# The opening of a fused transformer block: the silu(c) row read in PSUM, low parts made in pieces, and one written sequence for the queues

## The chip, the cores and the metric

The kernel runs on one NeuronCore of a Trainium2 chip (trn2). The metric is the device time of one execution in microseconds. Engines are named as in the profile: PE is the matrix engine (PEld its weight loads), DVE the vector engine, ACT the scalar engine, POOL the general one (GpSimd), and SP is the queue that issues the DMAs.

## The reference

One block on x of 2048 rows by 1024: a modulation from a conditioning row c, an attention with a memory over four segments of 512 rows (32 heads of 32), and a gated feed-forward of width 3584. All of it is float32.

```python
mod = (silu(c) @ w_mod).reshape(1, 6, 1, 1024)      # sa, ca, ga, sb, cb, gb
h = layernorm(x) * (1 + ca) + sa
q, k, v = h @ wq, h @ wk, h @ wv                    # 32 heads, 4 segments of 512
for s in range(4):
    p = softmax(qs @ ks.T * scale + mask)
    o = g * (phi(qs) @ M) / (phi(qs) @ z + 1e-6) + (1 - g) * (p @ vs)
    M, z = M + phi(ks).T @ vs, z + sum(phi(ks))
x = x + ga * (o @ wo)
h = layernorm(x) * (1 + cb) + sb
x = x + gb * ((gelu(h @ w_gate) * (h @ w_up)) @ w_down)
```

## The kernel before, in words

**Numbers.** Matrix products need more than one pass: an operand is split into a high part, rounded to the format of the fast pass, and a low part, the rest. A product is then high by high, low by high and high by low. ACT or DVE makes a high part with a cast, POOL or DVE makes the low part with a subtraction (on POOL in pieces of 256 columns).

**Stages.** The opening prepares segment 0 and projects it for the first group of four heads. Then come 33 steps of attention (for two halves, eight groups, two segments each), the output projection, and the feed-forward. In a step n the scores S of one group and segment are made, the second half T of the step before, and the projection K (keys and values) and Q of the step after. Inside a step a row of short names (`ORDER`) says in which sequence the pieces are written; all five queues take them in that sequence.

**The opening.** `modT` is a table of 48 columns of 128: column r = 8j + kt belongs to part j of the modulation (0 the shift sa, 1 the scale ca) and to the kt-th block of 128 channels. A column is made on DVE (`mod_col`, L159): w_mod's block r, 128 by 1024, times the row silu(c), spread over all partitions (`scb`), summed along the row; for a scale 1.0 is added (L164). The row itself is made by PE: ones times a diagonal of silu(c) (`row_parts`, L124 to L131), two halves in PSUM, copied by ACT to `scb`. Two of the 16 columns of the opening are made as products on PE instead (`mod_mm`, L170), from a block that the host has turned.

Segment 0 comes as x tiles of 128 rows. Their norm (`norm_stats`, L216 to L222: DVE's statistics, POOL's power -0.5; L1472 and L1475: the scaling on ACT) is followed by `norm_seg` (L311 to L329): for each kt PE turns four blocks into a PSUM bank (`tpa`), ACT makes h from it with the scale column and the shift column of this kt (L318), then come its high part `hha` and low part `hla`. `first_part` (L496, L499) takes kt after kt as they come and accumulates keys, values (`kv`) and queries (`q`) in three PSUM banks; it ends by copying them out (`kn` on ACT, `vx` on DVE), and by the pieces after it: `kt` turns the keys (kT) and splits them, `qo` splits the queries (qh, ql), `dk` and `dq` spread both by DMA into ks and qs, `ek`, `ea` and `eb` make phi.

Segment 1 does the same inside the opening's end and step 0. w_mod's blocks come in pairs (`pair(kt)`: scale and shift) into eight buffers, the first four pairs ahead of everything else, the others as buffers come free. Weights of the first group are rk, rq and rv; their high and low parts are w. The opening is recorded with its instructions in the written order on each queue. The 8 PSUM banks are: 2 for `mm`, 1 for `o`, 5 for `s` (turned blocks, scores, products of columns).

The opening's core, as written before:

```python
mod_col(*got[8])
scaled(0, 3, (0,), x0)
next(nseg)
mod_col(*got[0])
W[0][1] = split_w(raw0[1], wsp_tile("w0_1"), nc.vector)
next(nseg)
W[0][0] = split_w(raw0[0], wsp_tile("w0_0"))
...
for kt in range(1, KT + 1):
    ...
    (mod_mm if kt in (1, 7) else mod_col)(*got[8 + kt])
    mod_col(*got[kt])
    next(nseg)
```

Of the kernel before, what the change touches and what calls it, by code (L numbers as in the profile page):

```python
# [11 lines left out]
F32 = mybir.dt.float32  # L12
# [7 lines left out]
P = 128  # L20
D = 1024
# [15 lines left out]
def block_kernel(ctx: ExitStack, tc: tile.TileContext, x, c, wmod, wq, wkv, wo, beta, wg, wu, wd, out):  # L37
# [81 lines left out]
    def row_parts(dst, cols, tmp, name):  # L119

        dgs = []
        for h in range(2):
            dg = tmp(f"{name}dg{h}")
            nc.vector.tensor_tensor(dg.rearrange("p (k m) -> p k m", m=P), ident.unsqueeze(1).to_broadcast([P, 4, P]),  # L124
                                    cols[:, 4 * h:4 * h + 4].unsqueeze(2).to_broadcast([P, 4, P]), op=ALU.mult)
            dgs.append(dg)
        yield
        for h in range(2):
            ps = s_ps(f"{name}{h}")
            nc.tensor.matmul(ps, ones, dgs[h], start=True, stop=True)  # L130
            nc.scalar.activation(dst[:, h * L:(h + 1) * L], ps, AF.Copy)  # L131
            yield
# [25 lines left out]
    def mod_col(r, w, behind=False):  # L158
        i = nc.vector.tensor_tensor_reduce(out=w, in0=w, in1=scb, scale=1.0, scalar=0.0,  # L159
                                           op0=ALU.mult, op1=ALU.add, accum_out=modT[:, r:r + 1])  # L160
        if behind:
            hold(i)
        if r // 8 in (1, 4):
            nc.vector.tensor_scalar_add(modT[:, r:r + 1], modT[:, r:r + 1], 1.0)  # L164

    def mod_mm(r, w):

        ps = s_ps(f"col{r}")
        for k in range(KT):
            nc.tensor.matmul(ps[:, :1], w[:, k * P:(k + 1) * P], scol[:, k:k + 1], start=(k == 0), stop=(k == KT - 1))  # L170
        nc.scalar.activation(modT[:, r:r + 1], ps[:, :1], AF.Identity, bias=1.0)

# [10 lines left out]

    def load_w(src, name):
        return split_w(fetch(src, name), wsp_tile("w" + name))

# [115 lines left out]
    def norm_seg(s, halves):  # L302

        hs = hT[s] = []
        turned = []

        def turn(kt):
            if kt < KT:
                ps = s_ps(f"tpa{s}_{kt}")
                for i in range(4):  # L310
                    nc.tensor.transpose(ps[:, i * P:(i + 1) * P], halves[kt // 4][i][:, (kt % 4) * P:(kt % 4 + 1) * P], ident)  # L311
                turned.append(ps)

        turn(0)
        yield
        for kt in range(KT):
            h = tmp_tile(f"h{s}_{kt}")
            nc.scalar.activation(h, turned[kt], AF.Identity, bias=modT[:, kt:kt + 1], scale=modT[:, 8 + kt:9 + kt])  # L318
            hi = hT_tile(f"hha{s}_{kt}", s)
            lo = hT_tile(f"hla{s}_{kt}", s)  # L320
            if s:
                nc.vector.tensor_copy(hi, h)
            else:
                nc.scalar.activation(hi, h, AF.Copy)
            if s and kt % 2 == 0:
                nc.vector.tensor_sub(lo, h, f32(hi))
            else:
                for k in (0, L // 2):
                    nc.gpsimd.tensor_sub(lo[:, k:k + L // 2], h[:, k:k + L // 2], f32(hi[:, k:k + L // 2]))  # L329
            hs.append((hi, lo))  # L330
            turn(kt + 1)
            yield
# [148 lines left out]
    def first_part(n, g, s):  # L481
# [22 lines left out]
        yield  # L504
        for q in "kt dk ek qo dq ea eb".split():
            u[q]()
# [279 lines left out]
    def feed_forward():  # L786
# [547 lines left out]
        for m in range(NCH):  # L1334
# [33 lines left out]
        (0,):  # L1368
            "K N K G1 N K N K G2 N G0 K K S0 K S1 C1 K S2 l1 K C2 S3 L1 l2 tm tq A tr L2 K",
        (1,):  # L1370
            "T0 K0 K1 D0 ns K2 T1 rt nc P0 mz m0 nu dn K3 T2 n0 n1 o0 Q0 Q1 T3 nd S0 ne nl m1 P2 S1 rm S2 K4 "
            "Q2 S3 yt tm Q3 K5 K6 K7 tq wl qo o1 zs tr dq A kt ea eb dk ek",
# [46 lines left out]
    proj = projections()  # L1419
    gab = []  # L1420
    def opening():
        x0 = [[], []]
# [15 lines left out]
        def x1_load(i):  # L1438
            x1h.append(fetch(x[L + i * P:L + (i + 1) * P, :], f"x1_{i}"))

# [6 lines left out]
        pair(3)  # L1447
        x1_load(0)

# [39 lines left out]
        W[0] = [None, None, None]
        nseg = norm_seg(0, x0)  # L1490
        mod_col(*got[8])
        scaled(0, 3, (0,), x0)
        next(nseg)
        mod_col(*got[0])
        W[0][1] = split_w(raw0[1], wsp_tile("w0_1"), nc.vector)
        next(nseg)
        W[0][0] = split_w(raw0[0], wsp_tile("w0_0"))
        scaled(0, 0, (1,), x0)
        scaled(0, 1, (1,), x0)
        first = first_part(0, 0, 0)  # L1500
        nseg1 = None
        for kt in range(1, KT + 1):
            if kt < KT:
                if kt + 3 < KT:
                    pair(kt + 3)
                    if kt in (1, 2, 3):
                        x1_load(kt)
                (mod_mm if kt in (1, 7) else mod_col)(*got[8 + kt])
                mod_col(*got[kt])
                next(nseg)  # L1510
            if kt == 1:
                W[0][2] = split_w(raw0[2], wsp_tile("w0_2"))
                scaled(0, 2, (1,), x0)
                scaled(0, 3, (1,), x0)
            if kt == 3:
                x1h = [[t[:, h * L:(h + 1) * L] for t in x1h] for h in range(2)]
                nseg1 = norm_seg(1, x1h)
            if 3 <= kt < 7:
                stats(1, kt - 3, x1h)
            if 4 <= kt < 8:  # L1520
                scaled(1, kt - 4, (0, 1), x1h)
            next(first)
        next(nseg1)
        next(first)
        next(nseg1)
        next(nseg1)
        next(first)
        next(nseg1)
        next(nseg1)
        return x1h, nseg1  # L1530

# [146 lines left out]
```

## Time and profile before

| | us |
|---|---|
| median of 3 runs | 2776.51 (2775.17 to 2778.23) |
| the profiled execution | 2774.08 |
| its span, first to last instruction | 2772.4 |
| PE busy | 2725.8 |
| DVE, ACT, POOL busy | 1568.4, 1204.0, 888.9 |

A row of the timeline gives the start and the duration in us, the engine, the line, the operation, the tiles out<-in, the shape and how many instructions were merged; in brackets stands the idle time ahead of it and whose instruction ended it. A row of a table of windows gives the window, its length, then busy time (and count) of PE, PEld, DVE, ACT and POOL, the granted PE clock, the DMA share and GB/s. A row of a group gives count, busy time and mean ns, then idle time ahead. A row of a tile gives minimum, median and maximum in ns. A row of DMA issues gives the count, the size and the median us to landing.

### The profile page before, as it was taken

The page shows a single profiled execution, that of the slowest core. Times are in us where ns is not written, and L with a number is a line of the kernel's source. Part 1 is how long each engine was busy: PE and PEld are TensorE (multiplying, and loading weights), DVE is VectorE, ACT ScalarE, POOL GpSimd, SP SyncE. Part 2 cuts the span into 40 slices and gives each one's busy share as a digit, 9 for nine tenths or more (in the row PEclk, how much of TensorE's full clock was granted, in tenths as well). Part 3 has the DMA queues.
Part 4 walks back from the last instruction along what each step waited for, and adds up shares of the span by engine and source line. Part 5 has one row for each costly group of instructions (what it writes and reads, how often), then busy time and mean ns, then how long its engine had stood idle before and what let it go on. Part 6 is the DMA issues. An engine that isn't in the chain of part 4 may idle for free.

```text
span 2772.4 us, 43014 instructions
## 1 busy us (share of the span) xinstructions
PE 2725.8 (98%) x14748; PEld 2286.4 (82%) x14748; DVE 1568.4 (57%) x3519; ACT 1204.0 (43%) x2806; POOL 888.9 (32%) x1448
## 2 busy tenths in 40 slices
PE   7999999999999999999999999999999999999999
PEld 6798888888888777778888878888888888888887
DVE  7677667766676735655555445333433244475456
ACT  5677777776767624334322323111111033233323
POOL 5333334533333533344555552444351000000000
PEclk8999999999999999999999999999999999999999
DMA  6455444435443558778898778999999687796563
GB/s 228 135 147 151 113 145 137 134 100 147 121 130 100 149 183 273 243 293 302 321 340 322 267 267 279 341 362 362 353 361 329 215 303 264 259 307 207 179 206 127
DMA packets 244890, 637.77 MB, mean 230 GB/s; under 512 B 24768, under 2 KB 49344, under 8 KB 244672
## 3 DMA queue, kind: packets, MB, share of 16 engines
q1 hardware_dynamic: 244672, 635.03, 67.5%
q8 instruction: 116, 1.90, 0.3%
q14 instruction: 102, 0.84, 0.1%
HBM read 372.79 MB, written 211.81 MB: 211 GB/s over the span
## 4 chain that ended last, share of the span: by engine, by line
PE 89%; DVE 4%; issue 2%; POOL 2%; DMA 1%; ACT 1%; SPq 0%; POOLq 0%; ACTq 0%; DVEq 0%
PE f L1107 35%; PE y L1306 19%; PE kv L367 12%; PE q L373 6%; PE y L690 4%; PE S L524 3%; PE T L615 3%; PE O L627 3%; PE num L583 1%; PE M L566 1%; PE tpb L250 0%; POOL t L827 0%; PE R L633 0%; PE kT L401 0%; PE kv L496 0%
## 5 line engine op out<-in xcount | busy, mean ns | idle before, releaser
L1107 PE MATMUL f<-A,B 128*128 128x512 f32 x4704 | 1075.0, 390 | 3.6 <-DVE c L1127 1.5
L1107 PEld LDWEIGHTS f<-A,B 128*128 128x128 f32 x4704 | 880.8, 188 | 190.8 <-DVE c L1119 2.8
L1306 PE MATMUL y<-B,L 128*128 128x512 f32 x2352 | 533.3, 389 | 0.0
L1306 PEld LDWEIGHTS y<-B,L 128*128 128x128 f32 x2352 | 441.4, 188 | 91.7
L528 ACT ACTIVATE sj<-sj,mm 128x384 f32<-128x384 f32 (+3 forms) x512 | 281.4, 552 | 52.6 <-DVE mm L526 52.0
L526 DVE CUSTOM_DVE_ANT_0 sj<-S,mask 128x384 f32<-128x384 f32 (+3 forms) x512 | 227.9, 488 | 109.7 <-PE S L524 85.5
L618 POOL TENSOR_SCALAR_AFFINE_SELECT pt<-pt 128x128 f32<-128x128 f32 x512 | 165.3, 345 | 295.0 <-ACT pt L617 288.4
L821 ACT ACTIVATE L<-X 128x512 fp32r<-128x512 f32 x168 | 105.8, 630 | 258.6 <-PE y L1306 167.9
L617 ACT ACTIVATE pt<-T 128x256 f32<-128x256 f32 (+3 forms) x512 | 182.0, 445 | 66.0 <-PE T L615 58.8
L367 PE MATMUL kv<-w,hhh 128*128 128x256 f32 x1024 | 199.6, 285 | 0.0
L823 DVE TENSOR_TENSOR L<-X,L 128x512 fp32r<-128x512 f32 x168 | 116.0, 692 | 146.2 <-ACT L L821 146.1
L1130 ACT ACTIVATE g<-g 128x512 f32<-128x512 f32 x56 | 35.3, 631 | 339.9 <-DVE g L1129 339.9
L358 POOL TENSOR_TENSOR w<-r,w 128x256 fp32r<-128x256 f32 x180 | 133.1, 771 | 155.3 <-ACT w L352 153.7
L367 PE MATMUL kv<-w,hha 128*128 128x256 f32 x896 | 177.0, 285 | 0.0
L1046 POOL TENSOR_TENSOR rw<-rw,gbb 128x256 f32<-128x256 f32 x112 | 91.6, 853 | 247.4 <-DMA rw<-wd 166.5
L367 PEld LDWEIGHTS kv<-w,hhh 128*128 128x128 f32 x1024 | 164.8, 191 | 1.4 <-issue 0.4
L367 PEld LDWEIGHTS kv<-w,hha 128*128 128x128 f32 x896 | 145.6, 191 | 2.0 <-issue 0.8
L367 PE MATMUL kv<-w,hlh 128*128 128x256 f32 x512 | 144.7, 283 | 0.0
L690 PE MATMUL y<-wo,hho 128*128 128x512 f32 x384 | 125.7, 394 | 1.7 <-DVE xr L694 1.7
L367 PE MATMUL kv<-w,hla 128*128 128x256 f32 x448 | 126.9, 283 | 0.0
L1123 ACT ACTIVATE g<-f 128x512 f32<-128x512 f32 x56 | 33.5, 598 | 206.5 <-PE f L1107 206.5
L615 PE MATMUL T<-qs,ks 128*128 128x256 f32 (+2 forms) x512 | 108.3, 334 | 7.5 <-DVE qs L543 4.6
(244 smaller groups left out, 4215.4 us busy)
## 6 DMA issues: line engine op xcount, KB each, us to landing
bc_d<-B SPq DMA_DIRECT2D x189, 512.0 KB, 5.4
B<-bc_d SPq DMA_DIRECT2D x189, 512.0 KB, 5.4
B<-wc_d SPq DMA_DIRECT2D x112, 512.0 KB, 3.8
hid_d<-g SPq DMA_DIRECT2D x56, 512.0 KB, 4.3
wc_d<-T SPq DMA_DIRECT2D x56, 512.0 KB, 7.0
X<-hid_d SPq DMA_DIRECT2D x112, 256.0 KB, 4.9
wr<-gd_d SPq DMA_DIRECT2D x84, 256.0 KB, 4.0
ks<-kh SPq DMA_DIRECT2D x64, 256.0 KB, 3.6
```

Source lines behind the costliest of these rows:

```text
L358: nc.gpsimd.tensor_sub(w[:, 1, c], r[:, c], f32(w[:, 0, c]))
L367: nc.tensor.matmul(ps, b[:, sl], w[:, a], start=(kt == 0 and a == 0 and b is hi), stop=(kt == KT - 1 and a == 1), **kw)
L373: nc.tensor.matmul(ps, w[:, a], b, start=(kt == 0 and a == 0 and b is hi), stop=(kt == KT - 1 and a == 1), **kw)
L526: nc.vector.tensor_tensor_reduce(out=sj[:, :nv], in0=ps[:, :nv], in1=mask[:, L - nv:], scale=-1.0, scalar=3.4e38, op0=ALU.add, op1=ALU.min ...
L528: nc.scalar.activation(sj[:, :nv], sj[:, :nv], AF.Exp, bias=mm[:, j, i:i + 1], scale=-1.0, accum_out=ll[:, i, j:j + 1])
L615: nc.tensor.matmul(ps[:, :nn], ks[:, j, kc * P:(kc + 1) * P], qs[:, j, L - nn:], start=True, stop=True)
L617: nc.scalar.activation(pt, ps[:, nn - n:nn], AF.Exp)
L618: nc.gpsimd.affine_select(pt[:, :P], pt[:, :P], pattern=[[1, P]], compare_op=ALU.is_ge, fill=0.0, base=0, channel_multiplier=-1)
L690: nc.tensor.matmul(ps, b[:, i * P:(i + 1) * P], w[:, a, g % 2], start=(g == 0 and a == 0 and b is hi), stop=(g == G - 1 and a == 1))
L823: eng.tensor_sub(lo[:, k], src[:, k], f32(hi)[:, k])
L1107: nc.tensor.matmul(ps, B[m, i][:, a, kt * P:(kt + 1) * P], A[p, i, kt][b], start=(start and kt == 0 and a == 0 and b == 0), stop=(kt == 3 ...
L1306: nc.tensor.matmul(banks[t], ops[k][:, y, t * P:(t + 1) * P], B[slots[k]][:, x], start=(i not in (2, 4, 3) and j == 0 and x == 0 and y == ...
```

## The change

Seven things change, all in the opening and steps 0 and 1.

- The row silu(c) stays in PSUM as well: `scp`, two banks. `mod_col` reads it there for the opening's 16 columns (r below 16). ACT still copies it to `scb`, which the later columns read.
- For this the `s` banks are 3 in the opening; at the unit `S` the two banks are given back and `s` has 5 again.
- The low parts of wq's and of the value half's weights are written in pieces (`split_parts`), each a unit of its own.
- The opening is one written sequence of units, `OPENING`, with a name for each: `s` and `t` statistics, `a` and `b` scaling, `r` the row, `C` and `c` a scale and a shift column, `K`, `q`, `v` the weights' splits, `p` and `x` loads, `n` and `N` a kt of `norm_seg` for segment 0 and 1, `F` a kt (or end) of `first_part`.
- The columns made as products on PE are r = 6 and 15, where they were 9 and 15; the first x tile of segment 1 is loaded later.
- In segment 1, ACT makes the high parts of kt 0, 2, 3, 4 and 6 (DVE made all eight), and DVE the low parts of kt 0, 1, 5, 6 and 7 (it made 0, 2, 4 and 6).
- Step 0 has another row in `ORDER`, step 1 has `K0` ahead of `T0`, and the pieces after a `first_part` stand in another order (`AFTER`).

```diff
+    small = [*psum_pool("begin"), 3]
+    scp = small[0].tile([P, D], F32, name="scp")
     def s_ps(name):
-        return psum.tile([P, L], F32, name=name, tag="s", bufs=5)
+        return small[0].tile([P, L], F32, name=name, tag="s", bufs=small[2])
+
+    def s_all():
+        small[1]()
+        small[:] = [*psum_pool("small"), 5]
+        ctx.callback(small[1])
...
-            ps = s_ps(f"{name}{h}")
+            ps = scp[:, h * L:(h + 1) * L] if name == "sc" else s_ps(f"{name}{h}")
...
     def mod_col(r, w, behind=False):
-        i = nc.vector.tensor_tensor_reduce(out=w, in0=w, in1=scb, scale=1.0, scalar=0.0,
+        i = nc.vector.tensor_tensor_reduce(out=w, in0=scp if r < 16 else w, in1=w if r < 16 else scb, scale=1.0, scalar=0.0,
...
+    def split_parts(r, w):
+        nc.scalar.activation(w[:, 0], r, AF.Copy)
+        yield
+        for k in range(0, 1024, 256):
+            nc.gpsimd.tensor_sub(w[:, 1, k:k + 256], r[:, k:k + 256], f32(w[:, 0, k:k + 256]))
+            yield
...
-            if s:
+            if kt in HI_DVE[s]:
...
-            if s and kt % 2 == 0:
+            if kt in LO_DVE[s]:
...
-        for q in "kt dk ek qo dq ea eb".split():
+        for q in AFTER[s].split():
...
         (0,):
-            "K N K G1 N K N K G2 N G0 K K S0 K S1 C1 K S2 l1 K C2 S3 L1 l2 tm tq A tr L2 K",
+            "N K K N G1 K N N G2 K G0 K S0 S1 C1 S2 K S3 C2 K l1 l2 A tm tr tq L1 K K L2 K",
...
+    AFTER = ('qo kt ek dq ea dk eb', 'kt qo ea eb dk dq ek')
+    HI_DVE = ((), (1, 5, 7))
+    LO_DVE = ((), (0, 1, 5, 6, 7))
+    BY_PRODUCT = (6, 15)
+    OPENING = (
+        "s0 s1 a2 r r s2 a5 r q s3 a6 a4 a0 c0 C1 C0 K q n n a3 v p4 c1 q q C2 c3 c2 n p5 v C4 C3 F c5 n F q "
+        "c4 F x0 v p6 p7 v a7 a1 C5 n v x1 t0 C6 n n F x2 c6 n x3 C7 c7 b0 t1 t2 F F n b1 F t3 F b2 S b3 F F "
+        "N N N N N ")
```

On POOL, from the last norm of segment 0 to the low part of kt 4, this stood before (`w_0` from rq and `w_2` from rv are the weights, `rsa` a norm's power, x2 and x4 count pieces):

```order
L222 TENSOR_TENSOR rsa_3_230<-rsa_3_230,mhalf 128x1
L329 TENSOR_TENSOR hla_0_253<-h_0_250,hha_0_252 128x256 x2
L181 TENSOR_TENSOR w_0_262<-rq_141,w_0_262 128x256 x4
L329 TENSOR_TENSOR hla_1_288<-h_1_285,hha_1_287 128x256 x2
L181 TENSOR_TENSOR w_2_297<-rv_145,w_2_297 128x256 x4
L378 MEMSET vx_0_306 128x4x2
L378 MEMSET vx_1_668 128x4x2
L329 TENSOR_TENSOR hla_2_336<-h_2_333,hha_2_335 128x256 x2
L329 TENSOR_TENSOR hla_3_370<-h_3_367,hha_3_369 128x256 x2
L222 TENSOR_TENSOR rsa_0_384<-rsa_0_384,mhalf 128x1
L329 TENSOR_TENSOR hla_4_410<-h_4_407,hha_4_409 128x256 x2
```

And this stands there now:

```order
L200 TENSOR_TENSOR w_0_187<-rq_145,w_0_187 128x256
L345 TENSOR_TENSOR hla_0_260<-h_0_257,hha_0_259 128x256 x2
L200 TENSOR_TENSOR w_0_187<-rq_145,w_0_187 128x256 x2
L345 TENSOR_TENSOR hla_1_283<-h_1_280,hha_1_282 128x256 x2
L200 TENSOR_TENSOR w_2_189<-rv_149,w_2_189 128x256
L394 MEMSET vx_0_300 128x4x2
L345 TENSOR_TENSOR hla_2_324<-h_2_321,hha_2_323 128x256 x2
L200 TENSOR_TENSOR w_0_187<-rq_145,w_0_187 128x256
L200 TENSOR_TENSOR w_2_189<-rv_149,w_2_189 128x256 x2
L345 TENSOR_TENSOR hla_3_380<-h_3_377,hha_3_379 128x256 x2
L200 TENSOR_TENSOR w_2_189<-rv_149,w_2_189 128x256
L238 TENSOR_TENSOR rsa_0_397<-rsa_0_397,mhalf 128x1
```

The eight pieces of weights have been spread among the low parts of h; the low part of kt 2 stands behind four of them where it stood behind all eight.

On DVE, this stood from scale column 2 on (each column is an ISA row with its read of the sum behind it; a TENSOR_SCALAR follows a scale column only):

```order
L159 ISA wm_c,modT<-wm_c,scb 128x1024
L159 ISA modT 128x1
L164 TENSOR_SCALAR modT<-modT 128x1
L159 ISA wm_c,modT<-wm_c,scb 128x1024
L159 ISA modT 128x1
L159 ISA wm_d,modT<-wm_d,scb 128x1024
L159 ISA modT 128x1
L164 TENSOR_SCALAR modT<-modT 128x1
L159 ISA wm_d,modT<-wm_d,scb 128x1024
L159 ISA modT 128x1
```

And now, from the same column on:

```order
L171 ISA wm_c,modT<-scp,wm_c 128x1024
L171 ISA modT 128x1
L176 TENSOR_SCALAR modT<-modT 128x1
L171 ISA wm_d,modT<-scp,wm_d 128x1024
L171 ISA modT 128x1
L171 ISA wm_c,modT<-scp,wm_c 128x1024
L171 ISA modT 128x1
L171 ISA wm_a,modT<-scp,wm_a 128x1024
L171 ISA modT 128x1
L176 TENSOR_SCALAR modT<-modT 128x1
L171 ISA wm_d,modT<-scp,wm_d 128x1024
```

The shift column 3 (`wm_d` without an addition behind it) has moved ahead of shift column 2, and scale column 4 (`wm_a`) ahead of scale column 3.

On PE, at the end of step 0, the last scores stood directly ahead of the memory's sums M, the keys' turning kT and the first T:

```order
L524 MATMUL S_0_23_922<-ks_111,qs_0_635 128x512
L524 MATMUL S_0_33_927<-ks_111,qs_0_635 128x512
L566 MATMUL M_0_948<-vx_0_306,pk_0_629 128x130 x4
L401 MATMUL kT_1_962<-ident,kn_1_667 128x128 x4
L615 MATMUL T_0_00_992<-qs_0_635,ks_111 128x512
L615 MATMUL T_0_10_997<-qs_0_635,ks_111 128x512
```

Now M stands between the projections of kt 6 and kt 7 (`hla_6`, `hha_7`), which follow the last scores, and behind kT stands the first kv of the next projection:

```order
L515 MATMUL q_1_691<-hla_6_753,w_0_187 128x512
L582 MATMUL M_0_921<-vx_0_300,pk_0_610 128x130 x4
L512 MATMUL kv_1_0_689<-w_2_189,hha_7_763 128x256 x2
L512 MATMUL kv_1_1_690<-w_2_189,hha_7_763 128x256 x2
L515 MATMUL q_1_691<-hha_7_763,w_0_187 128x512
```

Two kt of projection have moved from ahead of the last scores to behind them, and K0 has moved ahead of T0.

More of the change, by code (lines that the diff above doesn't have):

```diff
@@ L58, in pool, with psum_pool @@
         return st.enter_context(tc.tile_pool(name=name, bufs=1, side=side, reuse_waits="tile")), st.close
+    def psum_pool(name):
+        st = ExitStack()
+        return st.enter_context(tc.tile_pool(name=name, bufs=1, space=PSUM)), st.close
     edge, edge_close = pool("edge", "right")
@@ L170, in mod_mm @@
             nc.tensor.matmul(ps[:, :1], w[:, k * P:(k + 1) * P], scol[:, k:k + 1], start=(k == 0), stop=(k == KT - 1))
-        nc.scalar.activation(modT[:, r:r + 1], ps[:, :1], AF.Identity, bias=1.0)
+        nc.scalar.activation(modT[:, r:r + 1], ps[:, :1], AF.Identity, bias=1.0 if r // 8 == 1 else 0.0)
     def split_w(r, w, eng=nc.gpsimd):
@@ L1447, in opening @@
         pair(3)
-        x1_load(0)
         nc.vector.memset(ones, 1.0)
@@ L1494, in opening @@
[L1494 to L1509, printed above, removed]
-                next(nseg)
[L1511 to L1522, printed above, removed]
@@ L1532, in attention @@
+        return nseg1[0]
     def attention(nseg1):
@@ L1655 @@
     wmod = np.array(np.asarray(w_mod).T.reshape(48, P, D))
-    for r in (9, 15):
+    for r in (6, 15):
         wmod[r] = np.asarray(w_mod)[:, r * P:(r + 1) * P].reshape(KT, P, P).transpose(1, 0, 2).reshape(P, D)
```

70 lines of the change are left out of this document (42 added, 28 removed).

## The prediction

> **What bounds the kernel now.** I read the page's first lines, then a table of windows, then TensorE's (PE's) rows up to its first full stretch, and last the rows of those it waits for.
>
> ```profile
> span 2772.4 us, 43014 instructions
> PE 2725.8 (98%) x14748; PEld 2286.4 (82%) x14748; DVE 1568.4 (57%) x3519; ACT 1204.0 (43%) x2806; POOL 888.9 (32%) x1448
> ```
> ```profile
> 20.00:25.00 5.00, 5.00 (x23) 4.90 (x24) 3.79 (x8) 4.51 (x8) 5.00 (x4) 0.50 1.03 409
> 30.00:35.00 5.00, 2.35 (x17) 1.89 (x16) 4.68 (x10) 1.41 (x2) 5.00 (x7) 1.00 1.03 411
> 35.00:40.00 5.00, 4.59 (x20) 4.06 (x21) 2.19 (x5) 1.52 (x2) 5.00 (x7) 0.66 1.00 392
> 40.00:45.00 5.00, 5.00 (x39) 4.68 (x38) 4.82 (x11) 2.93 (x4) 3.79 (x4) 1.00 0.05 17
> 95.00:200.00 105.00, 104.90 (x784) 91.33 (x783) 72.50 (x246) 82.17 (x234) 37.34 (x91) 1.00 0.54 149
> ```
> PE is busy for 98% of the span and idles 46.6 us in all. From 95 to 200 it idles 0.1 us, so a microsecond won ahead of 95 moves everything behind it. Ahead of 95 the table (PE, PEld, DVE, ACT and POOL busy, then granted clock, DMA share, GB/s) shows three limits: the loads, about 410 GB/s until 40 and then nothing; POOL, 5.00 of 5.00 from 20 to 40; and a clock granted at 0.50.
>
> ```profile
> 18.25 3.57 PE L170 MATMUL col<-scol,wm_b 128*128 128x1 f32 x16
> 22.43 1.20 PE L496 MATMUL kv<-w,hha 128*128 128x256 f32 x4
> 26.08 0.60 PE L311 MATMUL tpa<-ident,x 128*128 128x128 f32 x4
> 35.23 0.51 PE L496 MATMUL kv<-w,hla 128*128 128x256 f32 x2 [2.88 <-POOL hla L329]
> 45.86 1.84 PE L170 MATMUL col<-scol,wm_d 128*128 128x1 f32 x16
> 53.36 0.40 PE L499 MATMUL q<-hla,w 128*128 128x512 f32 x1
> 59.42 0.50 PE L499 MATMUL q<-hha,w 128*128 128x512 f32 x1 [2.57 <-DVE ql L434]
> 70.41 0.64 PE L496 MATMUL kv<-w,hha 128*128 128x256 f32 x4
> 74.67 0.64 PE L524 MATMUL S<-ks,qs 96*128 96x256 f32 x4
> 79.90 2.57 PE L524 MATMUL S<-ks,qs 96*128 96x384 f32 x8
> 85.42 0.63 PE L401 MATMUL kT<-ident,kn 128*128 128x128 f32 x4 [1.78 <-DVE mm L526]
> 90.66 2.07 PE L615 MATMUL T<-qs,ks 128*128 128x512 f32 x4 [4.61 <-DVE qs L543]
> 94.45 0.40 PE L367 MATMUL kv<-w,hha 128*128 128x256 f32 x2
> ```
> The projection of segment 0 ends at 53.8 (the q at 53.36), that of segment 1 runs on into step 0, and the first T with the K0 behind it (twelve kv) ends at 94.6. Two groups of one kt (kv and q, high and low) run from 70.41 to 74.67, 2.13 us each; the group from 22.43 to 26.08 took 3.65 at half clock. PE waits for POOL's low parts, for a PSUM bank (ql) and, last and longest, for DVE's end of step 0.
>
> **The change part by part.** *The row in PSUM.* A column of the modulation is one DVE instruction with two sources in SBUF; now one of them lies in PSUM.
>
> ```profile
> 14.08 1.22 DVE L159 CUSTOM_DVE_ANT_0 wm_a<-wm_a,scb 128x1024 f32<-128x1024 f32 x1
> 15.22 0.08 DVE L159 DVE_READ_ACCUMULATOR2_ANT modT<- 128x1 f32 x1
> 24.98 1.75 DVE L159 CUSTOM_DVE_ANT_0 wm_d<-wm_d,scb 128x1024 f32<-128x1024 f32 x1
> 75.00 0.29 DVE L526 CUSTOM_DVE_ANT_0 sj<-S,mask 128x128 f32<-128x128 f32 x1 [5.23 <-PE S L524]
> 81.35 0.55 DVE L526 CUSTOM_DVE_ANT_0 sj<-S,mask 128x384 f32<-128x384 f32 x1
> 81.30 2.79 POOL L358 TENSOR_TENSOR w<-r,w 128x256 fp32r<-128x256 f32 x4 [10.02 <-ACT w L352]
> L181 POOL TENSOR_TENSOR w<-rq,w x4: 722/1724/1773, 21.5 to 25.6; 128x256 fp32r<-128x256 f32 x4
> ```
> The same custom instruction with S in PSUM took 0.29 us for 128 elements and 0.55 for 384: 0.13 per 128, so 1.20 for 1024, against 1.22 today. Beside it POOL's pieces ran at 0.70 each (2.79 for four); beside the columns they took up to 1.77, and a column up to 1.75. The bounds are nothing won on either engine, or all of it; I take the near row, which has one source in PSUM: 1.15 from column to column (14.08 to 15.22), 1.35 where 1.0 is added, 0.72 for a piece on POOL. [...]
>
> *Loads.* They are the same bytes, with the x tiles of segment 1 behind most columns.
>
> ```profile
> 19.51 1.45 DVE L159 CUSTOM_DVE_ANT_0 wm_b<-wm_b,scb 128x1024 f32<-128x1024 f32 x1 [0.51 <-DMA wm_b<-wmod]
> 22.15 1.22 DVE L159 CUSTOM_DVE_ANT_0 wm_c<-wm_c,scb 128x1024 f32<-128x1024 f32 x1 [1.18 <-DMA wm_c<-wmod]
> wm_d<-wmod SPq DMA_DIRECT2D x4, 512.0 KB, 8.5
> ```
> 512 KB (0.524 MB) at 410 GB/s take 1.28 us; these two waits, two loads apart (1.32 each), agree. Continued from C2 at 22.15 (C a scale column, c a shift, the number its kt): c2 23.4, C3 24.7, c3 26.0, C4 27.2, c4 28.5, C5 29.8, c5 31.1, first x 32.3, C6 33.6, c6 34.9, C7 36.2, c7 37.5, the other x 38.7, 40.0, 41.3. A load needs its buffer: C6 and c6 wait on SP for the column c2, C7 and c7 for C3, which end at 28.3 and 31.0 (below): 5 us ahead, against 8.5 in a full queue and far less in one that has emptied; I count no delay, and 3.5 as the bound.
>
> *DVE.* Three of the four norms of segment 0 now stand ahead of the first column, with POOL's power awaited for two of them. So the first column starts near 17 instead of 14.08, and PE's first kv near 23.5 instead of 22.43. That is swallowed where c3, which stands ahead of c2, waits for its load: c3 26.0 to 27.15, c2 28.3, C4 29.65, C3 31.0, c5 (landed 31.1) 32.25, c4 33.4, C5 34.75, the norm of an x tile (1.28 and small rows, 1.65) 36.4, C6 37.7.
>
> ```profile
> 28.34 1.28 DVE L216 BATCH_NORM_STATS2 sta<-rx 128x6 f32<-128x512 f32 x2
> 33.27 0.78 ACT L318 ACTIVATE h<-tpa,modT 128x512 f32<-128x512 f32 x1 [3.31 <-DVE modT L159]
> 34.08 0.63 ACT L324 ACTIVATE hha<-h 128x512 fp32r<-128x512 f32 x1
> ```
> h and its high part take 1.45 us, POOL's two low pieces 1.45 more. h_2 starts at 28.35 and kt2 at 29.8, while before h_4 started only at 33.27. *The low parts in pieces*: POOL makes as many pieces as before in the order of use, so hla_2 is ready at 31.3, three pieces of weights at 33.4, hla_3 at 34.85, and PE has ended kt3 at 35.6.
>
> *Products and banks.* c6 is made on PE in place of C1, as many instructions; each product takes 1.84. With three s banks instead of five, the product of C7 gets its bank only when h_6 has been read (37.7 + 0.8): it runs from 38.6 to 40.4. kt4 to kt7, 4 x 2.13, end at 48.9; POOL has hla_7 by 45, which covers them, and PE waits if that fails by more than 3 us. From 35.6 to 40.4 PE runs little but products. Those at 18.25 left the clock at 0.50 (the window from 20 to 25, with kv from 22.43), so I add 3.4 us at half speed, 1.7: **segment 0 ends at 50.6 instead of 53.8**.
>
> *Segment 1 and step 0.*
> ```profile
> 53.32 0.66 ACT L384 ACTIVATE kn<-kv 128x256 f32<-128x256 f32 x2 [0.60 <-PE kv L496]
> 56.05 0.64 ACT L412 ACTIVATE ek<-kn 128x512 f32<-128x512 f32 x1
> L528 ACT ACTIVATE sj<-sj,mm 128x128 f32<-128x128 f32 (+3 forms) x16 | 8.8, 549 | 7.5 <-DVE mm L526 7.5
> L352 ACT ACTIVATE w<-r 128x1024 fp32r<-128x1024 f32 x2 | 2.1, 1042 | 0.0
> 87.14 0.17 DVE L534 CAST mt<-mm 128x16 fp32r<-128x16 f32 x1
> 88.91 1.69 DVE L543 TENSOR_SCALAR qs<-tt,seli 32x512 fp32r<-32x512 f32 x4
> ```
> Now kT, the kn ahead of it and q's parts come at once, ahead of the transposes. On ACT stand kn (0.66), qh, kh and ek (up to 0.64 each), h_0 and its high part (1.45): 3.9 us with overlap, beside which PE transposes. kt0 starts at 54.5, with ql long done, so the 2.57 us wait is gone. kt0 to kt4 and two sets of transposes of 0.4 end at 65.9. S0, S1 and S2 now stand in a row; each S beyond the fifth needs a bank that DVE frees at ACT's pace, so I put 3.0 us for 2.0 of work: 68.9. Then kt5 71.0, S3 72.3, kt6, M (about 0.9) and kt7: 77.4.
>
> Beside it ACT's 16 exponentials (8.8) and one cast (1.0) run from 66.5 to 76.3; DVE, three tiles ahead, ends its last maximum near 74.85, then Mt and the reciprocals (0.75), and as before 3.46 from mt to the end of qs (87.14 to 90.60): 79.1. kn waits for ACT's second cast, vx stands behind qs on DVE and K0 behind vx: K0 79.6 to 81.05, T0 to 82.0. So of what PE waited at the end (1.78 + 4.61, and T0 at half clock) some 2 us stay; the rest lies under kt6, M and kt7. On SP the spread of qs now goes ahead of that of ks, 12 us before S0 needs either. Five casts of segment 1 go from DVE to ACT (0.63 each), and POOL has one pair fewer: no cost, since ACT does little from 58 to 65; without that cover it would be 3 us.
>
> *Sum.* T0 with K0 ends at 82.0 instead of 94.6: **12.5 us** won, 3.2 in segment 0 and 9.3 behind it. From step 1 on the rows are the same but for K0 ahead of T0. 2774.08 - 12.5 = 2761.6 for an execution like the profiled one; the median of the runs shown lies 2.4 above that one, so 2764.0.
>
> **The rivals.**
> *The clock stays full over the products.* 1.7 us more: 14.2, 2762.3. For it, the product at 45.86 stands inside busy rows and the clock stayed at 1.00 there; against it, the window from 20 to 25. [...]
>
> *POOL is not freed.*
> ```profile
> L329 POOL TENSOR_TENSOR hla<-h,hha 128x256 fp32r<-128x256 f32 x16 | 16.2, 1039 | 6.4 <-ACT hha L324 6.4
> ```
> At today's means, 16 of these (1.04), 7 pieces of weights (1.35) and three powers (0.97) take 29 us from 23 on and end near 52: segment 0 ends as now, and some 8 to 9 us behind it stay: 2768. Against it: 2.79 for four beside L526.
>
> *The gain is handed back.* Step 1 has K0 first, which needs low parts that POOL makes only from 76.7 to 81, and C6 to c7 may come late. If such waits cost PE 7 us or more, 2771 to 2776. No row of step 1 shows slack that small; 3.5 us for late loads alone leave 9.
>
> *Slower.* A column of 1024 reads over two PSUM banks, which no row does. Thirteen columns lie between 17.0 and the end of C6, with 4.0 us of other rows: 17.0 + 13X + 4.0. At X over 2.25 us C6 ends after 50.2 and the whole 12.5 is gone; at 2.6 it is 2781. The near rows say 1.20.
>
> **How the numbers follow.** Forecast 0.55, clock full 0.12, POOL not freed 0.15, handed back 0.10, slower 0.08. A measurement tells about 0.2%, 5.6 us, from no change: faster 0.82, same 0.10, slower 0.08. The range leaves out the last two; it goes from the full clock, with the scatter of the runs (2 us) below it, 2760, to POOL not freed with the same above, rounded up to 2771.
>
> **What would show it.** Right: pieces on POOL at 0.72, columns near 1.2, h_2 near 28, C6 near 37.7, no wait of PE over 2 us for hla, the first kT near 51, T0 near 81. Wrong: columns near 2; pieces still at 1.7; T0 behind 88; or new waits of PE between 95 and 200.

## The result, and the profile after

The changed kernel took 2764.48 us (median of 5 runs, 2763.07 to 2768.4) against 2776.54 for the kernel before (5 runs). The ratio is 0.9958, with a 95% interval of 0.9943 to 0.9972. The forecast was 2764.0, in a range of 2760 to 2771. The profiled execution took 2763.21 us, 10.9 less than the one before. So the median lies 0.5 us from the forecast, while the profiled execution won 10.9 us of the 12.5 that were forecast for it.

The page's first lines, and the table of windows with the same columns as before:

```profile
span 2761.5 us, 43009 instructions
PE 2722.3 (99%) x14748; PEld 2283.1 (83%) x14748; DVE 1566.3 (57%) x3516; ACT 1207.0 (44%) x2811; POOL 875.2 (32%) x1446
```
```profile
20.00:25.00 5.00, 5.00 (x22) 4.67 (x22) 4.18 (x9) 4.62 (x7) 2.53 (x4) 1.00 1.03 410
30.00:35.00 5.00, 5.00 (x41) 4.75 (x40) 4.54 (x11) 3.67 (x7) 5.00 (x8) 1.00 1.03 410
35.00:40.00 5.00, 5.00 (x41) 4.95 (x41) 4.90 (x12) 3.28 (x7) 3.72 (x7) 0.88 0.98 391
40.00:45.00 5.00, 5.00 (x30) 4.62 (x30) 3.87 (x14) 4.63 (x8) 4.11 (x7) 0.78 0.02 7
80.00:85.00 5.00, 5.00 (x28) 4.61 (x28) 4.42 (x10) 2.85 (x5) 2.19 (x7) 0.68 1.01 228
95.00:200.00 105.00, 104.90 (x789) 92.91 (x788) 76.73 (x257) 82.05 (x232) 35.12 (x80) 1.00 0.55 158
```

PE is busy for 5.00 of 5.00 in every row from 30 to 45, where it had 2.35 and 4.59 before. From 95 to 200 it idles 0.1 us, as it did: no new waits came behind the opening. From 30 on the clock drops in two places, behind the products (0.88, then 0.78) and at the end of step 0 (0.68). The 1.00 in the first row is no gain: four kv took 1.22 us at 22.45 (below), as long as at 39.31, where the granted clock was 0.50 (39 to 42), while four take 0.65 at full clock (25.18). So PE ran at half speed there as in the kernel before, and the column doesn't show it.

TensorE's timeline through those places (L182 is a product of a column, L512 and L515 a projection's kv and q, L417 the turning of the keys, L383 the K0, L631 the T, L649 the first R of step 1):

```profile
22.45 1.22 PE L512 MATMUL kv<-w,hha 128*128 128x256 f32 x4
...
35.17 1.84 PE L182 MATMUL col<-scol,wm_c 128*128 128x1 f32 x16
37.34 2.10 PE L182 MATMUL col<-scol,wm_d 128*128 128x1 f32 x16
39.31 1.20 PE L512 MATMUL kv<-w,hha 128*128 128x256 f32 x4
...
48.98 0.39 PE L515 MATMUL q<-hla,w 128*128 128x512 f32 x1
49.38 0.71 PE L417 MATMUL kT<-ident,kn 128*128 128x128 f32 x4
...
76.57 0.71 PE L417 MATMUL kT<-ident,kn 128*128 128x128 f32 x4 [0.87 <-ACT kn L400]
79.22 0.39 PE L383 MATMUL kv<-w,hha 128*128 128x256 f32 x1 [1.93 <-DVE vx L401]
...
81.48 1.88 PE L631 MATMUL T<-qs,ks 128*128 128x512 f32 x4
...
86.77 0.60 PE L649 MATMUL R<-ident,rx 128*128 128x128 f32 x4
```

Segment 0 ends at 49.4 (53.8 before) and T0 with the K0 ahead of it at 83.4 (before, with K0 behind T0, at 94.6). Two kT rows and the R serve as marks below: kT of segment 0, kT of segment 1, and the first R of step 1, which began at 98.14 before and begins at 86.77 now. The gain at this last mark is 11.4 us, so all of the gain lies ahead of it (the steps behind it took 0.5 us more).

What DVE and POOL do there, in rows of the timeline and in groups of lines (up to 60 us, mean ns behind the busy time):

```profile
36.20 1.22 DVE L171 CUSTOM_DVE_ANT_0 wm_c<-scp,wm_c 128x1024 f32<-128x1024 f32 x1
75.62 3.09 DVE L559 TENSOR_SCALAR qs<-tt,seli 32x512 fp32r<-32x512 f32 x4
75.73 4.95 POOL L374 TENSOR_TENSOR w<-r,w 128x256 fp32r<-128x256 f32 x6 [4.73 <-ACT w L368]
```
```profile
L345 POOL TENSOR_TENSOR hla<-h,hha 128x256 fp32r<-128x256 f32 x22 | 16.3, 767 | 16.3 <-ACT hha L340 16.3
L200 POOL TENSOR_TENSOR w<-rq,w 128x256 fp32r<-128x256 f32 x4 | 2.9, 734 | 1.3 <-ACT w L197 1.3
...
L171 DVE CUSTOM_DVE_ANT_0 wm_b<-scp,wm_b 128x1024 f32<-128x1024 f32 x4 | 4.9, 1222 | 0.4 <-DMA wm_b<-wmod 0.4
```

A column with the row in PSUM takes 1.22 us, though POOL works beside it. POOL's pieces of weights take 0.73 to 0.75 where they took 1.22 to 1.49 (the same groups in the kernel before, below), and its idle time now ends with ACT's high parts: POOL is no longer behind.

```profile
L181 POOL TENSOR_TENSOR w<-rq,w 128x256 fp32r<-128x256 f32 x4 | 5.8, 1486 | 0.0
L181 POOL TENSOR_TENSOR w<-rv,w 128x256 fp32r<-128x256 f32 x4 | 4.8, 1219 | 0.0
```

One row was not foreseen. The four qs of DVE took 3.09 us, against 1.69 before, and they lie under POOL's row of six pieces, which starts 0.1 us later.

### The profile page after: what moved, and what is told of

It is laid out like the page before. It is cut to its first block, busy times and chain, and to the rows that moved or that the text cites. A ratio compares the mean times of both kernels' runs of the same rounds, so it can differ in the third digit from the quotient of the medians.

```text
span 2761.5 us, 43009 instructions
## 1 busy us (share of the span) xinstructions
PE 2722.3 (99%) x14748; PEld 2283.1 (83%) x14748; DVE 1566.3 (57%) x3516; ACT 1207.0 (44%) x2811; POOL 875.2 (32%) x1446
## 4 chain that ended last, share of the span: by engine, by line
PE 88%; issue 3%; DVE 3%; DMA 3%; POOL 2%; ACT 1%; SPq 0%; POOLq 0%; ACTq 0%; DVEq 0%
PE f L1123 35%; PE y L1322 19%; PE kv L383 12%; PE q L389 6%; PE S L540 3%; PE T L631 3%; PE O L643 3%; PE y L706 2%; PE num L599 1%; PE M L582 1%; POOL t L843 1%; PE kv L512 1%; PE kT L417 0%; DMA ra<-h_d 0%; PE R L649 0%
## 5 line engine op out<-in xcount | busy, mean ns | idle before, releaser
L383 PE MATMUL kv<-w,hhh 128*128 128x256 f32 x1024 | 199.6, 285 | 0.0
L383 PE MATMUL kv<-w,hha 128*128 128x256 f32 x896 | 177.3, 285 | 1.9 <-DVE vx L401 1.9
L383 PEld LDWEIGHTS kv<-w,hhh 128*128 128x128 f32 x1024 | 164.8, 191 | 1.4 <-issue 0.4
L383 PEld LDWEIGHTS kv<-w,hha 128*128 128x128 f32 x896 | 145.8, 192 | 4.1 <-DVE vx L401 2.2
L383 PE MATMUL kv<-w,hlh 128*128 128x256 f32 x512 | 144.7, 283 | 0.0
L383 PE MATMUL kv<-w,hla 128*128 128x256 f32 x448 | 127.0, 283 | 0.0
L631 PE MATMUL T<-qs,ks 128*128 128x256 f32 (+2 forms) x512 | 108.1, 333 | 2.9 <-ACT pt L633 2.7
```

The source lines that it names most:

```text
L383: nc.tensor.matmul(ps, b[:, sl], w[:, a], start=(kt == 0 and a == 0 and b is hi), stop=(kt == KT - 1 and a == 1), **kw)
L631: nc.tensor.matmul(ps[:, :nn], ks[:, j, kc * P:(kc + 1) * P], qs[:, j, L - nn:], start=True, stop=True)
```

## The experiments

Times of one execution scatter by some us, so each trace is read at its marks too. Behind the first R, the rest of the span lay between 2674.3 and 2679.0 us in the fourteen profiled executions of this study; one time alone tells little under 4 us. Nearly all of this scatter arises in one stretch, where the attention ends and the output projection begins: the start of the same PE instruction, counted from R, differs by 0.4 us at most among the fourteen at 815 us behind R, and by 4.5 us at 900.

**The row read from SBUF again.** The rest of the change stays.

```diff
-        i = nc.vector.tensor_tensor_reduce(out=w, in0=scp if r < 16 else w, in1=w if r < 16 else scb, scale=1.0, scalar=0.0,
+        i = nc.vector.tensor_tensor_reduce(out=w, in0=w, in1=scb, scale=1.0, scalar=0.0,
```

> The changed kernel, but the columns of the opening read the row from its copy in SBUF again (two sources in SBUF). Marker: start of the first R of step 1 on PE, 98.14 us in the kernel before and 86.77 in the changed one. Theory (a row in PSUM leaves POOL free): columns up to 1.6 us and more, POOL's pieces of 256 columns at 1.2 to 1.7 instead of 0.72, segment 0 ends 2 to 4 us later than 49.2, marker 89 to 91. Rival (the written order alone makes the gain): marker within 0.5 of 86.8.

Measured: 2772.7 us (10 runs, 2769.92 to 2777.2), ratio to the kernel before 0.9991 [0.9981, 1.0]. The profiled execution is the longest of the ten; its R comes at 96.69. Groups of lines up to 60 us, and TensorE's waits over the whole span (us, times, longest):

```profile
L345 POOL TENSOR_TENSOR hla<-h,hha 128x256 fp32r<-128x256 f32 x16 | 17.7, 1127 | 6.5 <-ACT hha L340 6.5
...
L171 DVE CUSTOM_DVE_ANT_0 wm_b<-wm_b,scb 128x1024 f32<-128x1024 f32 x4 | 6.3, 1563 | 0.0
```
```profile
PE kv L512 <- POOL hla L345: 6.1, 5, 2.4
```

Both engines pay: low parts take 1.13 us instead of 0.77, columns 1.48 to 1.60 instead of 1.22, and PE waits 6.1 us for low parts. The cause is as forecast, but the size is not: the mark was to come at 89 to 91, and 8.2 us by the medians (7.0 against the changed kernel's second set below) are more than the theory's 2 to 4. Some 5 us of the 9.9 at the mark are the waits for low parts (6.1 instead of a wait of 0.87 for a high part). Some 3 us more are clock: 3.4 us at half behind the first two waits (2.43 and 1.16 us; 0.76 and 0.90 in the windows from 30 to 40), and 6.8 us at half behind the products (0.63 and 0.69 from 45 to 55), where the changed kernel's execution has 3.4.

**The row in PSUM alone**, in the kernel before (the same edit of `mod_col` with its banks).

> The kernel before with one part of the change: the row read in PSUM, three s banks until segment 0 is through; the old order of everything. Theory: POOL's pieces at 0.72, PE's 4.8 us of waits for hla fall under 1.5, segment 0 ends at 50 to 51 instead of 53.8, marker 94.5 to 95.5. Rival (without a new order POOL's relief is worth nothing, since norms and columns stand in turn on DVE): marker within 1 of 98.1.

Measured: 2772.73 us (10 runs, 2769.66 to 2775.89), 0.9983 [0.9974, 0.9993]; R at 93.78, 4.4 us earlier. Its kT of segment 0 comes at 50.74 instead of 54.91, POOL's pieces take 0.73 to 0.77, PE's 4.8 us of waits for low parts are gone, and the waits at ql (2.56) and at the end of step 0 (1.78 and 4.62) are all still there.

```profile
50.74 0.60 PE L413 MATMUL kT<-ident,kn 128*128 128x128 f32 x4
...
93.78 0.60 PE L645 MATMUL R<-ident,rx 128*128 128x128 f32 x4
```

**The old step in the changed kernel.** Step 0's and step 1's old rows in `ORDER`, the old pieces behind a projection, the old shares of high and low parts, and the old order of segment 1 at the end of `OPENING`; the fence shows the pieces and the shares.

```diff
...
-    AFTER = ('qo kt ek dq ea dk eb', 'kt qo ea eb dk dq ek')
-    HI_DVE = ((), (1, 5, 7))
-    LO_DVE = ((), (0, 1, 5, 6, 7))
+    AFTER = ('kt dk ek qo dq ea eb', 'kt dk ek qo dq ea eb')
+    HI_DVE = ((), tuple(range(8)))
+    LO_DVE = ((), (0, 2, 4, 6))
...
```

> The changed kernel with the old rows of steps 0 and 1, the old order behind a first part and the old shares of ACT, DVE and POOL in segment 1. Theory (the order of step 0 is worth what the trace shows behind segment 0, 6.8 us): marker 93 to 94, the waits of 2.6, 1.8 and 4.6 us of PE back. Rival (most of it follows from segment 0 ending earlier): marker under 89.

Measured: 2772.98 us (10 runs, 2769.55 to 2777.05), 0.9986 [0.9977, 0.9995]; R at 91.80. TensorE's timeline shows the old waits:

```profile
54.77 0.50 PE L515 MATMUL q<-hha,w 128*128 128x512 f32 x1 [2.56 <-DVE ql L450]
...
79.25 0.63 PE L417 MATMUL kT<-ident,kn 128*128 128x128 f32 x4 [1.79 <-DVE mm L542]
...
84.49 2.07 PE L631 MATMUL T<-qs,ks 128*128 128x512 f32 x4 [4.62 <-DVE qs L559]
```

These three waits (9.0 us) become 0.87 and 1.93 in the changed kernel, which is the main part of what the step gives. The mark lies ahead of the forecast 93 to 94: the old step costs 5.0 us there, not 6.8.

**The new step alone**, in the kernel before: the same tables the other way round.

> The kernel before with the new rows of steps 0 and 1, the new order behind a first part and the new shares in segment 1, the old opening and the row in SBUF. Theory (the halves add up): marker 91 to 92, segment 0 ending at 53.8 as before. Rival (the new step needs the new opening): marker over 95.

Measured: 2770.69 us (10 runs, 2767.73 to 2772.68), 0.9975 [0.9965, 0.9984]; R at 90.92, 7.2 us earlier. It is the largest single part.

**Row and step together, the opening's order as before.** Neither the written sequence nor the pieces of weights.

> The row in PSUM and the new step, with the opening's loop and pieces as before. If the gains add up (4.4 for the row alone, 7.2 for the step alone, from 98.14), the first R of step 1 comes at 86.6 and the time is about that of the changed kernel, 2764 to 2765: the written sequence of the opening and the pieces of weights then carry nothing. The rival is that the sequence carries what the row with the sequence had over the row alone (6.3 against 4.4): the marker comes at 88.5 and the time is about 2 us longer, 2766 to 2767.

Measured, in one set with the changed kernel again:

> The changed kernel as it is, so that the next three can be compared with it on one chip. No theory moves it: a median of 2763 to 2766, the first R of step 1 near 86.8 in an opening whose kt2 does not wait.

2765.43 us (5 runs, 2762.65 to 2766.92), 0.9959 [0.9946, 0.9973], against 2765.70 (5 runs, 2764.42 to 2766.96), 0.9961 [0.9948, 0.9973] for the changed kernel on the same chip. TensorE's timeline of the kernel with row and step:

```profile
47.62 0.71 PE L413 MATMUL kT<-ident,kn 128*128 128x128 f32 x4
...
74.87 0.72 PE L413 MATMUL kT<-ident,kn 128*128 128x128 f32 x4 [0.87 <-ACT kn L396]
...
85.06 0.60 PE L645 MATMUL R<-ident,rx 128*128 128x128 f32 x4
```

The gains add up: 98.14 - 4.4 - 7.2 = 86.5, and R came at 85.06, 1 to 1.7 us ahead of the changed kernel's two executions (86.01 and 86.77). By the medians, each against the kernel before in its own set, they add up too: 4.3 and 6.3 us, against 10.2 together. So the written sequence, with its pieces of weights and its other choice of products, carries nothing that five runs can tell. Without the row in PSUM it costs: step and sequence (2772.7) stand 2.0 us behind the step alone (2770.69), and PE waits 6.1 us for low parts there against 4.5. (No wait of PE there is for a bank, so its three `s` banks don't explain it.) The new order lives on a POOL that is free.

**No column as a product.** All sixteen on DVE; the host turns no blocks.

```diff
-    BY_PRODUCT = (6, 15)
+    BY_PRODUCT = ()
```

> The changed kernel with no column made on PE: c6 and C7 are columns on DVE like the rest. Theory (PE's clock drops because products hardly count as work): kt4 runs at full clock, 2.1 us instead of 3.5, PE has 3.9 us less to do, DVE two columns more (1.2 and 1.35), and POOL's low parts become what kt4 to kt7 wait for: segment 0 ends near 46 instead of 49.2; ACT, which still scales x until 47, lets the keys go out only then: marker 84.5 to 85.5. Rival (the drop of the clock has another cause): kt4 again at half clock, marker over 86.

Measured (one run): 2769.25 us, R at 90.23, 3.5 us later and not earlier. Rows of its timeline, of ACT and of TensorE, and its window:

```profile
46.95 2.93 ACT L1499 ACTIVATE rx<-rx,mr,rsa 128x512 f32<-128x512 f32 x4 [0.30 <-DVE mr L1496]
...
50.20 1.11 PE L417 MATMUL kT<-ident,kn 128*128 128x128 f32 x4 [2.36 <-ACT kn L400]
51.10 5.22 PE L327 MATMUL tpa<-ident,rx 128*128 128x128 f32 x24
```
```profile
50.00:55.00 5.00, 4.80 (x23) 4.80 (x24) 4.29 (x9) 4.51 (x9) 0.00 (x0) 0.50 0.59 148
```

Segment 0 does end earlier here, at 47.8, and the clock stays at 1.00 from 30 to 45, where the products had been (0.88 and 0.78 from 35 to 45 with them). But DVE has two columns more, so the norms of segment 1 come late; ACT scales their tiles from 46.95 to 49.88 and makes kn only then; PE waits 2.36 us and then runs at a clock of 0.50 (the 24 turns take 5.22 us instead of 2.78). The theory had named the two columns and ACT's scaling, but put the end of the scaling at 47, and the half clock behind PE's wait was not in it. Of the clock it is one execution: one of eight with the products stayed at 1.00 too (below), so this does not show that the products lower it.

**The cut of weights later in step 0.** In `ORDER`, the piece that makes POOL's next low parts of weights moves behind the end of DVE's work.

```diff
-            "N K K N G1 K N N G2 K G0 K S0 S1 C1 S2 K S3 C2 K l1 l2 A tm tr tq L1 K K L2 K",
+            "N K K N G1 K N N G2 K G0 K S0 S1 C1 S2 K S3 K l1 L1 A tm tr tq K K C2 l2 K L2",
```

> The changed kernel, but the second cast of the next weights (C2) and its low parts (l2, L2) stand behind the keys' copy, and L1 directly behind l1. Theory (POOL's pieces lengthen DVE's four qs from 1.7 to 3.1 us, and vx and K0 wait for them): qs 1.7 us, K0 at 77.8 instead of 79.2, marker 85.2 to 85.6. Rival (something else lets K0 go): marker within 0.3 of 86.8.

> The step in which no cut of weights by POOL lies beside qs, now in rounds. If the collision of qs with POOL's pieces costs 1.4 us, qs takes 1.7 for its four and the median is 1 to 2 us under the changed kernel's on the same chip. The rival, that other waits take its place (K0 behind vx, low parts late in step 1), gives the changed kernel's time within 0.5 us.

Measured: 2766.72 us in one run, with R at 87.37 although its kT of segment 0 came only at 52.84; then, in a set of five, 2763.41 us (5 runs, 2763.09 to 2764.76), 0.9953 [0.9941, 0.9966], which is 2.3 us under the changed kernel on the same chip, and the best time of the study. Its timeline (DVE, POOL, PE), of the profiled execution of the set:

```profile
77.15 1.69 DVE L559 TENSOR_SCALAR qs<-tt,seli 32x512 fp32r<-32x512 f32 x4
...
79.35 3.05 POOL L374 TENSOR_TENSOR w<-r,w 128x256 fp32r<-128x256 f32 x4 [5.46 <-ACT w L368]
79.36 0.39 PE L383 MATMUL kv<-w,hha 128*128 128x256 f32 x1 [0.53 <-DVE vx L401]
...
85.37 0.60 PE L649 MATMUL R<-ident,rx 128*128 128x128 f32 x4
```

With no piece of POOL beside them the four qs take 1.69 us again, and the wait for vx is 0.53 instead of 1.93. From the second kT to R it takes 7.26 us, against 10.20 in the changed kernel: 1.4 is the shorter wait, the other 1.5 the clock behind the longer gap (0.68 from 80 to 85 there, 1.00 here).

**Low parts of the weights all at once**: the four pieces of each weight stand together on POOL, so that the low part of kt2 stands behind all eight.

> The changed kernel, but the four low pieces of each weight stand together on POOL as before. Theory (pieces near their use count even with POOL free): hla_2 stands behind all eight pieces, near 32.4 instead of 31.0, kt3 ends 1 to 1.5 us later, marker 87.5 to 88.3. Rival (with the row in PSUM POOL has time enough): marker within 0.3 of 86.8.

Measured (one run): 2767.48 us, R at 89.13, later than either forecast. PE waits only 0.5 us for low parts up to segment 0's end (0.3 for those of a weight, 0.2 for those of h). Its first product starts at 37.44, behind a kt2 at half clock (0.66 from 30 to 35), and the clock falls for longer behind the products (0.56 and 0.76 from 40 to 50); but an execution of the opening with its pieces (the late cut's first) shows the same, 37.06 and 3.1 us. So this run shows no worth of the pieces, in line with the kernel of row and step; it can't rule out a small one.

**Columns in the order of their loads.** The columns c2, C3, c3, C4 and c5 stand as their blocks land.

```diff
-        "s0 s1 a2 r r s2 a5 r q s3 a6 a4 a0 c0 C1 C0 K q n n a3 v p4 c1 q q C2 c3 c2 n p5 v C4 C3 F c5 n F q "
-        "c4 F x0 v p6 p7 v a7 a1 C5 n v x1 t0 C6 n n F x2 c6 n x3 C7 c7 b0 t1 t2 F F n b1 F t3 F b2 S b3 F F "
+        "s0 s1 a2 r r s2 a5 r q s3 a6 a4 a0 c0 C1 C0 K q n n a3 v p4 c1 q q C2 c2 n p5 v C3 c3 F C4 n F q "
+        "c4 F x0 v p6 p7 v a7 a1 C5 n v x1 c5 t0 C6 n n F x2 c6 n x3 C7 c7 b0 t1 t2 F F n b1 F t3 F b2 S b3 F F "
```

> The changed kernel with the columns of kt 2 to 5 in the order in which their loads land. Theory (the loads bound PE up to the products): h_2 starts 1.2 us earlier and PE doesn't wait 0.9 us at kt2, but the product of c6 then waits for its load, marker 86.4 to 86.9. Rival (DVE's order bounds it): everything behind moves with it, marker 85.7 to 86.0.

Measured (one run): 2766.24 us, R at 86.45. PE no longer waits ahead of kt2, and waits for a load five us later instead:

```profile
34.75 1.92 PE L182 MATMUL col<-scol,wm_c 128*128 128x1 f32 x16 [0.88 <-DMA wm_c<-wmod]
...
80.41 0.39 PE L383 MATMUL kv<-w,hha 128*128 128x256 f32 x1 [1.93 <-DVE vx L401]
...
86.45 0.60 PE L649 MATMUL R<-ident,rx 128*128 128x128 f32 x4
```

At the products a load sets the pace, as forecast. Here K0 and T0 ran at full clock (1.00 from 75 to 85) behind the same gap: 8.68 us from the second kT to R. That the mark fell into the forecast is in part luck: this execution lost 3.2 us of clock behind the products and none at K0, where the changed kernel's first lost 1.5 at each.

**Both orders together.**

> The late cut, and the columns of kt2 to kt5 in the order in which their loads land. The loads set the pace of the opening, so the order of columns should add nothing by the theory of loads: the late cut's time within 0.5 us. The rival is that a column waiting for its load holds up kt2 (the wait of PE ahead of kt2, 0.87 to 2.3 us in different executions, and the half clock behind it): then another 1 to 3 us are won.

Measured: 2765.16 us (5 runs, 2764.24 to 2765.92), 0.9958 [0.9946, 0.9971]. Its R is the earliest of all, 84.29, and yet its time lies 1.8 us over that of the late cut alone. The gain at the mark is not the order's: the first product starts at 35.50 behind a wait of 1.06 us for its load, 0.4 us later than in the late cut's set of five, and the clock behind the products then cost 1.5 us less (next table). Behind R its profiled execution took 2.3 us more, and 2.2 of them arise between 840 and 900 us behind R, where PE has nearly the same two waits (2.66 and 1.95 us, against 2.67 and 2.29) but a lower clock. Two windows there, of both orders and then of the late cut:

```profile
925.00:935.00 10.00, 7.34 (x29) 5.18 (x31) 7.81 (x18) 6.28 (x13) 9.56 (x16) 0.76 0.89 257
975.00:985.00 10.00, 8.05 (x42) 5.79 (x41) 4.24 (x4) 2.11 (x2) 10.00 (x16) 0.83 0.22 81
```
```profile
925.00:935.00 10.00, 7.33 (x35) 6.05 (x33) 8.80 (x19) 6.29 (x12) 9.41 (x15) 0.85 0.88 236
975.00:985.00 10.00, 7.71 (x46) 5.55 (x45) 5.01 (x5) 2.11 (x2) 10.00 (x15) 1.00 0.23 81
```

So in these two executions the order of columns adds nothing ahead of R, as the theory of loads has it. Whether it costs the 1.8 us of the medians stays open.

**The clock, over eight executions.** TensorE's instructions from the products up to the kT of segment 0 are the same, in the same order and without a wait, in eight traces. From the start of the first product to that kT they took:

| execution | product of c6 | kT of segment 0 | between | over the shortest |
|---|---|---|---|---|
| changed, again | 35.87 | 48.55 | 12.68 | 0 |
| changed, first | 35.17 | 49.38 | 14.21 | 1.5 |
| both orders | 35.50 | 49.79 | 14.29 | 1.6 |
| late cut, set of five | 35.12 | 50.91 | 15.79 | 3.1 |
| late cut, one run | 37.06 | 52.84 | 15.78 | 3.1 |
| low parts at once | 37.44 | 53.22 | 15.78 | 3.1 |
| order of loads | 34.75 | 50.59 | 15.84 | 3.2 |
| row from SBUF | 43.43 | 59.23 | 15.80 | 3.1 |

The windows of the first and the fourth row:

```profile
35.00:40.00 5.00, 5.00 (x45) 4.91 (x44) 4.89 (x13) 3.16 (x7) 4.07 (x7) 1.00 0.94 378
40.00:45.00 5.00, 5.00 (x37) 4.70 (x37) 4.13 (x13) 4.67 (x8) 4.22 (x8) 1.00 0.05 14
```
```profile
35.00:40.00 5.00, 5.00 (x38) 5.00 (x36) 4.90 (x12) 2.87 (x5) 3.55 (x7) 0.78 0.97 385
40.00:45.00 5.00, 5.00 (x22) 4.71 (x23) 3.90 (x13) 4.62 (x8) 3.96 (x7) 0.54 0.01 4
```

Behind the same products the clock fell in seven executions of eight, at a loss of 1.5 to 3.2 us, and in one not at all. The windows tell for how long. The fourth row's 0.78 and 0.54 are 0.22 and 0.46 short of full, over 5 us each: 3.4 us of clock, or 6.8 us at half. The changed kernel's first, with 0.88 and 0.78 above, was at half for 3.4 us. By the same sum over their windows the five executions with losses of 3.1 and 3.2 have 6.8 us at half, and the two with 1.5 and 1.6 have 3.4. The products alone don't decide it: with a single one, at 40 us, the clock fell for 6.8 us in the row alone (0.66 in both windows from 40 to 50) and stayed at 1.00 in the kernel of row and step. At the end of step 0 the clock varied in the same way behind the gap ahead of K0: the stretch from the second kT to R took 10.20 us, or 8.68 where the clock stayed, behind the same waits of 0.87 and 1.93. What decides it in one execution is open.

## Why the prediction was right, and where it was not

*The row in PSUM: right in kind, and its size too.* Columns were to take near 1.20 us and pieces 0.72; they take 1.22 and 0.73 to 0.77. Nothing was dearer for reading PSUM: the column at 14.08 in the kernel before, with both sources in SBUF, took 1.22 as well. Alone it gives 4.4 us at the mark.

*Loads and DVE: right.* C6 was to end at 37.7 and ended at 37.4; the first column near 17 started at 16.65; c3 waited 1.16 us for its load, which swallowed the later start, as the step had it. PE's first kv, put near 23.5, came at 22.45 already. That a load takes far less in an emptied queue has a row too: `na`, 512 KB, issued at 68.14 in the kernel before, landed after 3.6 us, against 8.5 for `wm_d`.

*Products and banks: the wait did not come.* The step put the product of C7 at 38.6, behind the reading of h_6. It started at 37.34, because ACT's reading of c6's product had freed a bank by then (37.05, 0.17 us): 1.3 us too dear. The clock was put at 1.7; it cost 1.5 in the profiled execution and 0 to 3.2 over eight. The ground given for this term does not hold: the product at 18.25 did not leave the clock at 0.50, for in the kernel before it was there already ahead of it:

```profile
15.00:16.00 1.00, 0.33 (x1) 0.14 (x1) 0.72 (x5) 0.03 (x2) 0.70 (x1) 0.71 1.05 418
16.00:17.00 1.00, 0.15 (x1) 0.15 (x2) 1.00 (x1) 1.00 (x2) 0.00 (x0) 0.50 1.05 418
```

Nor does a row of the kernel before show the 3.4 us at half speed that make the 1.7; the windows of the eight executions show 0, 3.4 and 6.8. That the size came so near is luck. With the wait for a bank gone, segment 0 ended at 49.4 instead of 50.6. Over the four executions of this same opening its kT stood at 48.55, 49.38, 50.91 and 52.84, mean 50.4: as a typical value the forecast was close.

*Segment 1 and step 0: 2.3 us too much.* From the end of segment 0 the step put kt7's end 26.8 us later; it came 26.3 later. K0 was put 29.0 behind it and came 29.85; T0's end 31.4 and came 34.0. Two terms failed. The first took the 3.46 from mt to the end of qs over from before, but the new order puts POOL's cut of weights beside qs, and qs grew by 1.4 us; the late cut shows it by taking it away. The second let K0 and T0 run at full clock ("K0 79.6 to 81.05, T0 to 82.0"); behind the gap the clock was lower (0.68 from 80 to 85), 1.5 us. Beside POOL's pieces the four qs went from 1.69 to 3.09 us, while the columns with their row in PSUM stayed at 1.22; the forecast had asked what runs beside POOL for the columns only.

*The sum.* 4.4 in segment 0 (3.2 forecast) and 7.0 behind it (9.3): 11.4 instead of 12.5 at the mark. The two misses, 1.2 too little and 2.3 too much, partly cancel, and the median's 0.5 us owes something to the scatter of the executions.

*The part that the sum did not price.* The written sequence and the pieces were counted as the way in which the low parts come in time. The kernel with row and step alone is as fast, so they were not needed for it. This is a step of the reasoning that failed though the number held.

*The rivals.* "The clock stays full" did happen in one of eight executions, and its price of 1.7 lies within what the others lost (1.5 to 3.2). "POOL is not freed" was priced at 2768, on the ground that 8 to 9 us behind segment 0 would stay; the row read from SBUF gave 2772.7. The step's failing part is "segment 0 ends as now": in the profiled execution, the longest of its ten, the new order with a slow POOL ends it later than before (kT at 59.23 against 54.91), since PE waits 6.1 us for low parts and the clock falls behind these waits (0.76 from 30 to 35). "Handed back" and "slower" had no sign: 0.1 us idle from 95 to 200, columns at 1.22.

## What to carry to other kernels

Price an order together with the rates that it lives on, and test the parts crosswise: two parts gave all of this gain that can be measured, and the third adds nothing beside the first and costs without it. Where POOL's work is moved to a new place, look at what DVE does there, and at what its instructions read: columns with two sources in SBUF (1.48 to 1.60 us instead of 1.22) and the four qs (3.09 instead of 1.69) grew beside POOL, columns with one source in PSUM did not (1.22). Waits of PE near 3 us in all (0.87 and 1.93 here) cost half as much again in clock (1.5) in six executions of eight and nothing in two, so read stretches between marks in several traces, not one time.

## What the runs showed of the hardware

Instructions that kept PE busy by the profile (32 products of 128 by 1) were followed by a dropped clock in seven executions of eight, and in one by none. In the one execution without them it stayed at 1.00 from 30 to 45; that they are the cause is not shown. Behind the same instructions the losses were 0, 1.5 to 1.6 and 3.1 to 3.2 us, so the length of the drop differed from execution to execution. Behind PE's 0.87 and 1.93 us of waiting with a kT between, the clock fell in six of eight executions (the stretch took 10.2 us instead of 8.7).
